# Early log sums on TensorE, exponentials for three more chunks, half products and pairwise weight sums in a fused SSD and expert kernel

## The chip, the cores and the metric

The kernel runs on one core of a Trainium2 chip. The metric is the device time of one execution in microseconds. A core has TensorE (PE, matmuls into PSUM banks), VectorE (DVE), ScalarE (ACT), GpSimd (POOL) and SyncE (SP), which issues nearly all DMA transfers here. Each engine takes its instructions in program order and waits for semaphores of the others.

## The reference

Four batches with eight heads of 768 tokens go through a Mamba2 state-space layer (chunks of 32 in the reference). Its output, 3072 tokens of 256 values, goes through four experts whose outputs are weighted by normalised probabilities:

```python
for c in range(nc):
    cum = np.cumsum(log_a[:, :, sl], axis=-1)
    L = np.exp(cum[:, :, :, None] - cum[:, :, None, :]) * causal
    M = np.einsum('bhin,bhjn->bhij', Cc, Bc) * L
    y_intra = np.einsum('bhij,bhjd->bhid', M, xc)
    y_inter = np.einsum('bhin,bhnd->bhid', Cc, state) * np.exp(cum)[:, :, :, None]
    y[:, :, sl] = y_intra + y_inter
    decay_from_j = np.exp(cum[:, :, -1:] - cum)
    state = np.exp(np.sum(la, -1))[..., None, None] * state + np.sum(
        np.einsum('bhjn,bhjd->bhjnd', Bc, xc) * decay_from_j[..., None, None], axis=2)
# tokens (3072, 256); p = domain_probs / sum
for e in range(4):
    out += p[:, e:e + 1] * (np.maximum(x @ w1[e], 0) @ w2[e])    # w1 256x1024, w2 1024x256
```

## The kernel before

Everything is fp32. The sequence is cut into chunks of 128 tokens, 24 in all: chunk c belongs to batch c mod 4, so c = 0 to 3 are the first chunks of the four batches and carry no earlier state, and six chunks (three pairs) make a block of the expert stage, four blocks in all. For each chunk the kernel needs the decays L between all pairs of its tokens and per head, the scores C·B, their product MT, and then `inner` (L546), which multiplies MT with the chunk's values and at the same time makes the chunk's part of the state. `score` is L502.

Decays are made in two ways. `scan` (L519, DVE) multiplies the a's up along the tokens against an identity: every row starts at its own token. It is used for c < SCANNED = 6; for chunks 0 to 2 the a's are spread over the partitions by matmuls of ones (`spread`, L660), for 3 to 5 they are read from DRAM, broadcast, into `ab` (L463, from `acut_d`). From chunk 6 on `decay` (L526, ACT) takes exponentials of differences of running log sums: `ab` is then read from `cum_d`, the negated sums per partition are in `neg`, and `causal` (L531, POOL) clears the upper triangle. `fade` multiplies B with the decays to the chunk's end. The DVE multiplications of scores and decays are L681 in the opening and L856 later.

The experts are computed with fewer products than a plain matmul: the four weight blocks of an expert (256 hidden columns each) and two halves of the input against a block's three pairs of chunks by a scheme of 20 products (`G`) per expert and layer, a unit of the order, and a scheme of 7 (`B`) for the first block's pairs 1 and 2. The weight operands of a scheme are sums and differences of weight blocks (`operands`, L1024, on POOL or DVE), stored to DRAM when first made (`w_d`, L1029) and read back for later blocks. Token operands are L1043 sums; the middle step (relu and gate) is `gated` (L968); L1071 adds a kept term into a bank; L942 and L947 copy between banks and SBUF; L1213 saves output banks; L1260 and L1425 add output terms. All product matmuls are L933; a product with 256 columns is two matmuls, and a matmul leaves two records in the trace. The first chunk pair is multiplied plainly for the four blocks of expert 0 (`plain_first`), because weight sums are not ready yet.

The order of work is fixed when the program is built. The opening (until about 13 us) is written out by hand: chunks 0 and 1, gates, the store of `acut_d`, the loads of the first weights, the log sums by a scan over time (L725) and the store of `cum_d`. Behind it a planner (`Plan.run`) goes through TensorE's list of work in the order given and puts the other engines' work in order by estimated costs, with a choice of DVE or POOL for sums and with SP's DMA issues. Constants such as `now = 13.2` and the ready times in `plan.taken` tell it when the opening is over. `PAIRS_AT` says where in a block's units the next block's chunk pairs get their scores (s) and outputs (o). At the end the last block's output pieces are turned on TensorE (L1325) and written out.

## Time and profile before

| | |
|---|---|
| median of 3 runs | 612.55 us (612.52 to 612.58) |
| the profiled execution's own time | 612.72 us |
| its span, first to last instruction | 610.9 us |
| TensorE busy | 603.7 us, 3365 records |
| VectorE, ScalarE, GpSimd busy | 489.8, 292.9, 158.8 us |
| product matmuls L933 | 1676 + 692 + 208 records |
| POOL weight sums L1024, 128x256 | 94 + 32, 794 and 763 ns each |
| DMA moved | 99.65 MB, mean 163 GB/s |
| granted TensorE clock | 1.00 |

A row of the timeline has start, length, engine, line, operation, tiles written and read, shape, count, and in brackets how long the engine stood idle before it and what ended that. Matmul records overlap; spacing between starts tells more than the length of one.

### The profile page before, as it was taken

What the parts mean: (1) busy time and instruction counts of PE and PEld (TensorE: products, weight loads), DVE (VectorE), ACT (ScalarE), POOL (GpSimd) and SP (SyncE); (2) the same over time, 40 slices, a digit from 0 to 9 for tenths busy, and PEclk for the clock granted to TensorE, in tenths of its full rate; (3) what the DMA queues carried; (4) which work ended last, traced back from release to release, by engine and by line L of the source; (5) the groups of instructions that cost most, each with busy time, mean ns of one, the idle gap of its engine ahead of it and who ended that gap; (6) DMA issues with size and microseconds to landing.
All of it is one profiled execution on the core that took longest, in us unless ns stands there. A gap on an engine that the chain in (4) does not pass through costs nothing.

```text
span 610.9 us, 10142 instructions
## 1 busy us (share of the span) xinstructions
PE 603.7 (99%) x3365; PEld 513.6 (84%) x3365; DVE 489.8 (80%) x854; ACT 292.9 (48%) x681; POOL 158.8 (26%) x238
## 2 busy tenths in 40 slices
PE   9999999999999999999999999999999999999997
PEld 5778778888888888888888888888888888888885
DVE  7899997988879894887969988396785989575775
ACT  5267365487642327868352334734444142434441
POOL 6565546556461001676400100200000000000000
PEclk9999999999999999999999999999999999999999
DMA  7757668566853429893332425863142232953001
GB/s 253 257 185 222 194 215 326 187 213 228 285 160 98 113 36 328 280 313 124 134 117 87 149 47 140 274 237 118 55 127 80 87 91 63 341 187 121 1 0 53
DMA packets 89060, 99.65 MB, mean 163 GB/s; under 512 B 27428, under 2 KB 58928, under 8 KB 89008
## 3 DMA queue, kind: packets, MB, share of 16 engines
q1 hardware_dynamic: 88852, 98.95, 51.3%
q8 instruction: 27, 0.44, 0.3%
q14 instruction: 25, 0.20, 0.1%
q10 hardware_dynamic: 156, 0.06, 0.0%
HBM read 78.80 MB, written 20.17 MB: 162 GB/s over the span
## 4 chain that ended last, share of the span: by engine, by line
PE 92%; DVE 2%; ACT 1%; issue 0%; DVEq 0%
PE bank L933 88%; PE bank L546 2%; PE bank L502 1%; PE bank L879 1%; ACT A L556 1%; DVE v L968 1%; DVE v L960 0%; DVE MT L856 0%; ACT v L894 0%; DVE bank L1071 0%; DVE v L1260 0%; PE bank L1325 0%; DVE v L1425 0%; ACT LT L894 0%; ACT v L1330 0%
## 5 line engine op out<-in xcount | busy, mean ns | idle before, releaser
L933 PE MATMUL bank<-v,w 128*128 128x256 f32 x1676 | 394.8, 380 | 0.8 <-DVE bank L1071 0.7
L933 PEld LDWEIGHTS bank<-v,w 128*128 128x128 f32 x1676 | 316.9, 190 | 48.2 <-issue 2.2
L933 PE MATMUL bank<-Y,w 128*128 128x256 f32 x692 | 177.6, 381 | 0.7 <-ACT LT L894 0.4
L1213 ACT COPY v<-bank 128x512 f32<-128x512 f32 x109 | 64.0, 587 | 178.5 <-PE bank L933 166.2
L933 PEld LDWEIGHTS bank<-Y,w 128*128 128x128 f32 x692 | 130.2, 190 | 22.4 <-issue 2.0
L968 DVE SCALAR_TENSOR_TENSOR v<-bank,gate 128x512 f32<-128x512 f32 x149 | 102.3, 688 | 42.6 <-PE bank L933 39.7
L960 DVE TENSOR_TENSOR v<-v,v 128x512 f32<-128x512 f32 x181 | 126.6, 719 | 1.7 <-ACT v L942 0.3
L1071 DVE TENSOR_TENSOR bank<-bank,v 128x512 f32<-128x512 f32 x84 | 57.4, 696 | 35.7 <-PE bank L933 23.4
L942 ACT COPY v<-bank 128x512 f32<-128x512 f32 x100 | 58.6, 587 | 54.0 <-PE bank L933 45.0
L1024 POOL TENSOR_TENSOR w<-w,w 128x256 f32<-128x256 f32 x94 | 73.1, 794 | 42.5 <-DVE v L960 14.5
L947 ACT COPY bank<-v 128x512 f32<-128x512 f32 x127 | 74.0, 595 | 10.7 <-DVE v L968 8.7
L933 PE MATMUL bank<-LT,w 128*128 128x256 f32 x208 | 52.7, 379 | 0.0
L526 ACT ACTIVATE MT<-ab,neg 128x128 f32<-128x128 f32 x144 | 47.1, 396 | 2.1 <-DMA ab<-cum_d 2.1
L933 PEld LDWEIGHTS bank<-LT,w 128*128 128x128 f32 x208 | 39.4, 190 | 5.3
L531 POOL TENSOR_SCALAR_AFFINE_SELECT MT<-MT 128x512 f32<-128x512 f32 x36 | 23.2, 655 | 69.2 <-ACT MT L526 53.9
L1024 POOL TENSOR_TENSOR w<-w 128x256 f32<-128x256 f32 x32 | 24.3, 763 | 18.8 <-DVE Y L1043 7.7
L960 DVE TENSOR_TENSOR v<-bank,v 128x512 f32<-128x512 f32 x26 | 17.9, 688 | 11.1 <-PE bank L933 9.9
L856 DVE TENSOR_TENSOR MT<-bank,MT 128x512 f32<-128x512 f32 x36 | 22.7, 681 | 0.1
L1260 DVE TENSOR_TENSOR v<-v,v 128x256 f32<-128x256 f32 x55 | 21.1, 422 | 1.0 <-ACT v L1213 0.7
L960 POOL TENSOR_TENSOR v<-v,v 128x512 f32<-128x512 f32 x6 | 7.7, 1277 | 49.7 <-DVE v L960 49.7
L968 DVE SCALAR_TENSOR_TENSOR v<-v,gate 128x512 f32<-128x512 f32 x26 | 19.8, 763 | 0.4
L495 ACT ACTIVATE ctm<-xb,tmask 128x128 f32<-128x128 f32 x48 | 15.8, 395 | 3.8 <-DMA xb<-in_xbc_dram 3.7
(110 smaller groups left out, 315.1 us busy)
## 6 DMA issues: line engine op xcount, KB each, us to landing
w<-w_d SPq DMA_DIRECT2D x128, 256.0 KB
w_d<-w SPq DMA_DIRECT2D x64, 256.0 KB
w<-in_w_dram SPq DMA_DIRECT2D x40, 256.0 KB
ab<-cum_d SPq DMA_DIRECT2D x18, 512.0 KB
w<-in_w_dram SPq DMA_DIRECT2D x64, 128.0 KB
gate<-p_d SPq DMA_DIRECT2D x15, 384.0 KB
xb<-in_xbc_dram SPq DMA_DIRECT2D x17, 192.0 KB
out_dram<-v SPq DMA_DIRECT2D x144, 16.0 KB
```

The source lines that it names most:

```text
L526: nc.scalar.activation(out=MT[:, place(c, h), 0:P], in_=ab[:, h * P:h * P + P], func=AF.Exp, bias=neg[:, h % NT, NQ * real(c) + h // NT:NQ ...
L531: nc.gpsimd.affine_select(out=MT[:, h:h + n, 0:P], in_=MT[:, h:h + n, 0:P], compare_op=ALU.is_ge, fill=0.0, base=0, pattern=[[0, n], [1, P ...
L856: nc.vector.tensor_mul(to, g, LT0[:, js, h] if cs[0] < SCANNED else to)
L933: nc.tensor.matmul(out=o, lhsT=w[:, j], rhs=x if half is None else x[:, j], start=(start and j == 0), stop=(j == 1), skip_group_check=True)
L942: act(.5, lambda e: nc.scalar.copy(out=flat(v), in_=bank.t), reads=[bank], writes=[v])
L947: act(.54 if to - lo > FB else .32, lambda e: nc.scalar.copy(out=bank.t[:, lo:to], in_=flat(v)[:, lo:to]), reads=[v], writes=[bank])
L960: plan.add(engines, lambda e: (on(e).tensor_add if sign > 0 else on(e).tensor_sub)(flat(v), whole(x), whole(y)), reads=[x, y], writes=[v], ...
L968: dve(D512, lambda e: nc.vector.scalar_tensor_tensor(out=h.t, in0=whole(x).rearrange("p (j m) -> p j m", j=JJ), scalar=0.0, in1=g.t[:, 2 * ...
L1024: plan.add(B256, lambda e, r=r, x=x, y=y, sign=sign: (on(e).tensor_add if sign > 0 else on(e).tensor_sub)(view(r), view(x), view(y)), two= ...
L1071: dve(D512, lambda e: (nc.vector.tensor_add if sign > 0 else nc.vector.tensor_sub)(to.t, bank.t, whole(x)), reads=[x, bank], writes=[to])
L1213: act(.5, lambda e: nc.scalar.copy(out=flat(v), in_=bank.t), reads=[bank], writes=[v], hold=HOLD)
L1260: plan.add(engines, lambda e: (on(e).tensor_add if sign > 0 else on(e).tensor_sub)(o[1](), x[1](), y[1]()), reads=[v for v in vs if v is n ...
```

## The change

It has four parts.

- Log sums early. The logarithm of `a` is taken right after the clipping; TensorE turns it (`sum_logs`), multiplies it with an upper triangle of ones (`upto`), which gives the running sums in both layouts, and ACT copies them to `cum` and, negated, to `neg`. The stores of `acut_d`, `p_d` and `cum_d` now stand together on SP ahead of the weights of blocks 2 and 3. The scan for the log sums and the later turn (`bias`, L1360) are gone.
- Chunks 2, 3 and 5 take their decays from exponentials; chunk 4 keeps its scan (`SCANS = 4,`). The triangle of the first four heads of chunks 2, 3 and 5 is cleared on DVE by a minimum with a mask of 2 and 0 (`bound`), the other four heads on POOL as before; `fade` of chunks 2 to 5 goes to DVE, by half chunks. `ab` has four buffers instead of two, the `v` pool 33 instead of 35. `spread` serves chunks 0 and 1 only, both at the start.
- `first_half`: for weight blocks 0 and 1 the first plain product is made per chunk, 128 columns at a time; chunk 0's part comes before chunk 1's `inner`. All four plain products stand ahead of the scores of chunks 2 and 3.
- Weight sums of two operands at a time: a pair of sums with a common layout is one instruction of 512 columns (7 pairs and 2 single ones instead of 16). For that the weights are loaded by input half with two blocks next to each other (`load_pair`).

Planner constants and the place of one pair's scores (24 to 18) are changed as well.

```diff
-NV, NW = 35, 28
+NV, NW = 33, 28
...
-SCANNED = 6
 SCORED, OWN, LEAD, LEFT = 7, 4, 5, 3
-FILLED = 3
-HORIZON, OPENING, LOADED = 26.0, 80.0, 1.0
+SCANS = 4,
+FILLED, EARLY, FADE = 3, 4, "DVE"
+CUT = {(c, 0): "DVE" for c in range(2, 6)}
+HORIZON, OPENING, LOADED = 26.0, 80.0, -0.5
 ORDERS = (0, 1, 2, 3), (3, 1, 2, 0), (0, 1, 2, 3), (3, 1, 2, 0)
-PAIRS_AT = ((1, 24, "s0"), (2, 1, "o0"), (2, 1, "s1"), (2, 24, "s2"), (3, 1, "o12")), (
+PAIRS_AT = ((1, 18, "s0"), (2, 1, "o0"), (2, 1, "s1"), (2, 24, "s2"), (3, 1, "o12")), (
...
-G.sums = ((15, 13, 10, -1), (9, 11, 10, -1), (0, "a", 16, -1), (2, "c", 11, -1), (1, "c", 13, -1),
-          (14, 16, 13, -1), (3, "e", 10, -1), (7, 10, "c", -1), (18, "d", 10, -1), (17, "d", 16, -1),
-          (8, 16, 11, -1), (19, "a", 13, -1), (6, "a", 11, -1), (12, 13, "d", -1), (5, "e", 16, -1),
-          (4, 11, "e", -1))
+G.ends = ("a", "c"), ("d", "e")
+G.sums = (((15, 9), (13, 11), 10), (0, "a", 16), ((1, 2), "c", (13, 11)), ((14, 8), 16, (13, 11)),
+          ((18, 3), ("d", "e"), 10), (7, 10, "c"), ((17, 5), ("d", "e"), 16),
+          ((19, 6), "a", (13, 11)), ((12, 4), (13, 11), ("d", "e")))
...
-    def causal(MT, h, n):
+    def causal(e, MT, h, n):
+        if e == "DVE":
+            nc.vector.tensor_tensor(
+                out=MT[:, h:h + n, 0:P], in0=MT[:, h:h + n, 0:P],
+                in1=bound.unsqueeze(1).to_broadcast([P, n, P]), op=ALU.min)
+            return
...
+    upto = const.tile([P, P], FP32)
+    nc.gpsimd.memset(upto, 1.0)
+    nc.gpsimd.affine_select(
+        out=upto, in_=upto, compare_op=ALU.is_ge, fill=0.0, base=0, pattern=[[1, P]],
+        channel_multiplier=-1)
...
+    def first_half(bank, w, y, c):
+        for i in range(2):
+            for j in range(JJ):
+                nc.tensor.matmul(
+                    out=bank.rearrange("p (a m) -> p a m", a=2)[:, j, c * P:c * P + P],
+                    lhsT=w1_half(w, i)[:, j], rhs=y[:, i, c * P:c * P + P],
+                    start=(c == 0 and i == 0 and j == 0), stop=(i == 1 and j == 1),
+                    skip_group_check=True)
...
+    def sum_logs(bank):
+        n = NCH * NH // 2
+        turned_ = homes["W"][-3][:, :2 * n].rearrange("p (r i) -> p r i", r=2)
+        nc.scalar.activation(out=a_sb, in_=a_sb, func=AF.Ln)
+        for r in range(2):
+            nc.tensor.transpose(bank[:, r * n:r * n + n], a_sb[:, r], ident[:n, 0, :n])
+        yield
+        nc.scalar.copy(out=turned_, in_=bank[:, :2 * n].rearrange("p (r i) -> p r i", r=2))
+        nc.tensor.matmul(
+            out=bank[:, 2 * P:2 * P + 2 * n], lhsT=upto, rhs=turned_.rearrange("p r i -> p (r i)"),
+            start=True, stop=True, skip_group_check=True)
+        for r in range(2):
+            nc.tensor.matmul(
+                out=bank[:n, r * P:r * P + P], lhsT=turned_[:, r], rhs=upto,
+                start=False, stop=True, skip_group_check=True)
+        yield
+        nc.scalar.copy(out=homes["cum"][1], in_=bank[:n, :2 * P].rearrange("p (r s) -> p r s", r=2))
+        yield
+        nc.scalar.mul(
+            homes["neg"][0], bank[:, 2 * P:2 * P + 2 * n].rearrange("p (r i) -> p r i", r=2), -1.0)
+        yield
...
+    logs, turning = sum_logs(four[0]), turn_gates(four[1])
     idle(BANK[6])
     idle(BANK[7], 3)
     spread(0, four)
-    idle(BANK[6], 3)
+    spread(1, seven, 1)
     mask(0, ctm[0], xb[0])
+    mask(1, ctm[1], xb[1])
     score([0], ctm[:1], xb[:1], seven)
-    scan_quarters(0, LT[0], four, 0)
+    scan_quarters(LT[0], four, 0, 0)
+    idle(four[1], 1)
+    next(logs)
+    next(turning)
     aside(0, 0, seven[0])
+    next(logs)
     aside(0, 1, seven[1])
-    scan_quarters(0, LT[0], four, 1)
-    fade(0, MT[0], xb[0], LT[0])
-    mask(1, ctm[1], xb[1])
-    spread(1, four)
+    next(turning)
+    next(logs)
+    store_decays(nc.sync, acut_d, a_cut)
+    nc.sync.dma_start(out=p_d.rearrange("e c s -> c e s"), in_=p_sb)
+    store_decays(nc.sync, cum_d, homes["cum"][1])
+    for fb in range(2, 4):
+        load_w1(fb, homes["W"][fb])
+    for fb in range(2):
+        load_w2(fb, homes["W"][4 + fb])
+    for c in range(2, 4):
+        load_decays(c, homes["ab"][c - 2])
+    for fb in range(2, 4):
+        load_w2(fb, homes["W"][4 + fb])
+    next(logs)
+    scan_quarters(LT[0], four, 0, 1)
     for r in (2, 3):
         masked(0, r, MT[0], LT[0], seven[r], 0)
-    turn_gates(BANK[7])
-    nc.scalar.activation(out=a_sb, in_=a_sb, func=AF.Ln)
-    next_ = [BANK[4], BANK[0], BANK[1], BANK[6]]
-    scan_quarters(1, LT[1], four, 0)
-    score([1], ctm[1:], xb[1:2], next_)
-    aside(1, 0, next_[0])
-    y = BANK[7][:, :NT * (P + N)].rearrange("p (t s) -> p t s", t=NT)
+    fade(0, MT[0], xb[0], LT[0])
+    idle(four[2], 3)
+    score([1], ctm[1:], xb[1:2], four, (2, 3, 1, 0))
+    scan_quarters(LT[1], seven, 1, 0)
+    aside(1, 1, four[1])
+    y = seven[0][:, :NT * (P + N)].rearrange("p (t s) -> p t s", t=NT)
     for t in range(NT):
         inner(0, t, y[:, t], xb[0], MT[0], P + N, t == 0)
     nc.scalar.copy(out=yT0[:, :, 0:P], in_=y[:, :, 0:P])
     keep_state(0, A[0], y[:, :, P:])
-    scan_quarters(1, LT[1], four, 1)
+    spread_gate(seven[1], homes["gate"][0])
+    scan_quarters(LT[1], seven, 1, 1)
+    for fb in range(2):
+        first_half(seven[2 + fb], homes["W"][fb], yT0, 0)
...
-    now = 13.2
+    now = 12.5
...
+    for c in range(2, 4):
+        st[c]["ab"] = plan.taken("ab", c - 2, now - 2.0 + 1.5 * c)
...
+        made, early = {}, c < blocks[0].n
+        for h in range(0, NH, NQ) if c in SCANS else ():
+            made[h] = dve(1.15, lambda e, h=h: scan(
+                LT0[:, j], s["ab"].t[:, h * P:h * P + NQ * P], place(c, h) * P),
+                reads=[s["ab"]], part=[LTv[place(c, h) // NQ]], two=True)
+        for h in range(NH) if c not in SCANS else ():
+            made[h] = act(.30, lambda e, h=h: decay(
+                c, s["MT"].t[:, j], s["ab"].t, neg.t, h),
+                reads=[s["ab"], neg], part=[s["MT"]])
+            if early and place(c, h) < NQ:
...
+            e = CUT.get((c, h), "POOL")
+            w = made[h] if c in SCANS else plan.add({e: .72 if early else .85}, lambda e, h=h: causal(
+                e, s["MT"].t[:, j], place(c, h), NQ), part=[s["MT"]], two=e == "DVE",
+                behind=[made[x] for x in range(h, h + NQ)])
+            cut.append(w)
+            to = [w]
+            if early:
+                e = FADE
+                to.append(plan.add({e: .3 if e == "POOL" else .2}, lambda e, h=h: fading(e, h, NQ),
...
+    def load_pair(v, fbs, l, f, i):
+
+        e, fb = divmod(fbs[f], EPB)
         if l == 1:
-            return w1[e, i * P:i * P + P, f * FB:f * FB + FB]
-        return w2[e, f * FB:f * FB + FB, i * P:i * P + P].rearrange("(j p) m -> p j m", p=P)
+            nc.sync.dma_start(out=v.t, in_=w1[e, i * P:i * P + P, fb * FB:fb * FB + 2 * FB])
+        else:
+            nc.sync.dma_start(
+                out=v.t.rearrange("p (j m) -> p j m", m=P),
+                in_=w2[e, fb * FB:fb * FB + 2 * FB, i * P:i * P + P].rearrange("(j p) m -> p j m", p=P))
...
+            for r, x, y in scheme.sums:
+                if isinstance(r, tuple):
+                    plan.add(B512, lambda e, r=r, x=x, y=y: difference(e, both(r), both(x), both(y)),
+                             two=True, reads=[where[x], where[y]], part=[where[r]], lean=True)
+                else:
+                    plan.add(B256, lambda e, r=r, x=x, y=y: difference(e, view(r), view(x), view(y)),
+                             two=True, reads=[where[x], where[y]], part=[where[r]], lean=True)
...
+        if fb < len(halves):
+            b = halves[fb]
+            seq = [plan.add({"PE": .44}, lambda e: first_half(b.t, w.t, y.t, 1), reads=[w, y], writes=[b])]
+            return seq, gated(b, gate_of(0, fb), 0)
...
-    for seq, _ in plain[:2]:
+    for seq, _ in plain[:EARLY]:
         line.extend(seq)
-    bias()
     scores([2, 3])
-    for seq, _ in plain[2:]:
+    for seq, _ in plain[EARLY:]:
```

## Prediction, made before the changed kernel had run

> **What bounds the kernel now.** I read the page's busy times first, then the stretches, then TensorE's waits, then the timeline of the first 30 us. The page:
>
> ```profile
> span 610.9 us, 10142 instructions
> PE 603.7 (99%) x3365; PEld 513.6 (84%) x3365; DVE 489.8 (80%) x854; ACT 292.9 (48%) x681; POOL 158.8 (26%) x238
> ```
>
> TensorE (PE) is the bound, so only what takes work or idle time out of its stream can show. The stretches (busy us by engine) and TensorE's waits after the opening:
>
> ```profile
> 0.00:12.60 12.60, 11.41 (x87) 5.99 (x87) 9.38 (x30) 5.94 (x17) 7.75 (x23) 1.00 0.73 229
> 12.60:26.30 13.70, 13.59 (x102) 10.99 (x99) 11.03 (x17) 4.44 (x15) 9.06 (x14) 1.00 0.86 280
> 60.00:80.00 20.00, 19.31 (x119) 15.62 (x122) 18.46 (x33) 7.77 (x23) 10.98 (x20) 1.00 0.66 206
> ```
> ```profile
> PE bank L1325 <- DVE v L1260: 0.7, 1, 0.7
> PE bank L933 <- DVE bank L1071: 0.7, 1, 0.7
> PE bank L933 <- ACT LT L894: 0.4, 1, 0.4
> ```
>
> Columns of the first: length, busy of PE, weight loads, DVE, ACT, POOL, granted clock, DMA share, GB/s. From 60 to 80 us VectorE (DVE) is busy 18.46 of 20 us: TensorE's losses there come from a full DVE queue. A product record (each fp32 product matmul leaves two) goes by every 0.216 us: groups of four start at 65.66, 66.53 and 67.39. Against that, the product runs lose about 1.0 us in all between 32 and 55 us in many small steps, 0.85 at 72 (the L1071 wait), 0.5 at 82 (the L894 wait), and 0.3 each at 123 and 232. From 233 us to the output's turns at 601 the stream is dense. So apart from the first 26 us some 3 us could be won.
>
> The beginning, from the timeline (start, length):
>
> ```profile
> 9.10 0.70 PE L546 MATMUL bank<-MT,xb 128*32 128x144 f32 x16
> 9.73 0.97 PEld L652 LDWEIGHTS bank<-p_sb,ident 96*128 96x128 f32 x8 [0.23 <-DVE LT L519]
> 10.82 1.21 PE L546 MATMUL bank<-MT,xb 128*32 128x144 f32 x16
> 11.21 0.47 SPq L463 DMA_DIRECT2D ab<-acut_d  x1
> 11.83 0.51 ACT L734 COPY v<-bank 128x128 f32<-128x128 f32 x2 [0.32 <-PE bank L546]
> 11.99 0.33 SPq L630 DMA_DIRECT2D cum_d<-cum  x1
> 12.61 3.72 PE L933 MATMUL bank<-v,w 128*128 128x256 f32 x16
> 16.16 0.33 PE L1360 MATMUL bank<-ident,cum 96*128 96x96 f32 x2
> 17.50 7.17 PE L933 MATMUL bank<-v,w 128*128 128x256 f32 x32
> 19.22 2.34 DVE L519 TENSOR_TENSOR_SCAN LT<-ab,ident 128x512 f32<-128x512 f32 x2 [2.06 <-DMA ab<-acut_d]
> 19.46 1.83 SPq L469 DMA_DIRECT2D ah<-cum_d  x3
> 24.68 1.69 PE L546 MATMUL bank<-MT,xb 128*32 128x144 f32 x32
> ```
>
> Chunk 1's own product ends near 11.9, ScalarE (ACT) copies it until 12.34, plain products run from 12.61. The loads are slow: `ab`, issued at 11.21, releases the scan at 19.22 (8.0 us); the `cum_d` store, issued at 11.99, releases its reader at 19.46 (7.4 us). Before `ab` the queue got 3.7 MB (eight weight tiles of 0.26, four chunks of 0.33, small ones of 0.3) and moved 229 GB/s at first.
>
> **The opening, part by part.** DVE's chain (eight scans of 0.6, five multiplications of 0.37, 4.68 to 11.30) keeps its length. New on TensorE, ACT and SP is the way to `cum_d` by logarithm, turn, triangular product and copy. The logarithm (0.42) overwrites what POOL still copies until 6.20: 6.25 to 6.7. Hand-overs ACT to PE take 0.26 (12.34 to 12.60), PE to ACT 0.35 from the last start (7.79 to 8.14). So: two turns 6.95, copy 7.4 to 7.7, product (a 192-column pass pair 0.33, four 96-row passes of 0.11) 8.0 to 8.7, copy 9.0 to 9.4, `cum_d` issued at 9.4 instead of 11.99, negated sums ready at 9.65. Chunk 1's scores now wait for those sums' bank: they end about 10.2 instead of 9.1, so chunk 0's product starts near 10.2, not 9.10. Its copy ends at 11.3. The first half products follow: eight passes of 128 columns each, by the L652 row 0.97/8 = 0.12 a pass, so 0.9 each, 1.8 for two: 11.5 to 13.3. Chunk 1's product 13.5 to 14.05, copies to 14.45, and the planned stream begins at 14.4.
>
> What TensorE then no longer has to do before the products of chunks 2 and 3: the turns at 16.16 (0.26) and 1.8 of plain products, done already. The `spread` of chunk 2 (11.96) lay under ACT's copy and its loss is worth nothing. The stream reaches L546 of chunks 2 and 3 after 0.9x2 + 16x0.216 (3.46) + scores 1.3 + 16x0.216 (3.46): 14.4 + 10.0 = 24.4, against 24.68. Without a wait it leaves at 25.5 (32 records in 1.12 later on, 1.62 here) instead of 26.30: 0.8 us at best.
>
> **The exponentials.** Chunks 2 and 3 now need `ab` from `cum_d`: store, landing, two loads of 512 KB behind four weight loads on SP's in-order queue. Of the store's 7.4 us now, 1.45 MB then in the queue (4.2 less 229x12.0) account for 4.4 at 330 GB/s; the other 3.0 stay. At 9.4 us here 229x9.4 covers the 2.1 MB issued, but the rate is lower at first, so 0.5 for a rest: the store is through at 12.9 and the loads follow; bounds 10.3 (0.5 after its issue) and 16.8 (7.4 again). Then ACT: four exponentials of chunk 2, four of chunk 3, chunk 3's mask, eight more; a run of five at L526 took 1.58 us, so 0.32 each, 1.3 for four. Behind T1, the landing of chunk 3's `ab`, lie 1.3 + 0.65 + 1.3 + 1.3 on ACT, POOL's L531 select 0.65, a fade on DVE 0.25, two multiplications 1.35 and TensorE's 1.16: 8.0 us. L546 leaves at T1 + 8.0. Bounds of T1: 3.2 MB lie ahead of the first load (six weight tiles, four chunks, 0.34 of small ones); by 12.6 us 229x12.6 = 2.9 MB have moved, the rest (0.3 MB plus two loads of 0.52) at 330 GB/s takes 4.1 us: data through at 16.7. (330 is 280 from 12.6 us on over a DMA share of 0.86.) The `ab` of before had 4.2 MB with its own, so by the same rates data through at 16.5, and it released its scan 2.7 later. T1 is 17.2 (tail 0.5, little more than a semaphore's hand-over) to 19.4 (tail 2.7), if the store does not hold the issue. I take 18.3, the middle, since the queue is shorter at the moment of issue (12.9): L546 leaves at 26.3, the 26.30 of now. Term: **0**, bounds -0.8 and +1.1.
>
> The Trainium skill (DMA: Bandwidth & Descriptors, Anatomy of one DMA) has a fixed cost of about 2 us plus bytes at 436 GB/s; by that the store would be through at 11.9, both loads by 16.4, and this term would be -0.8. Both rows above, 8.0 and 7.4 us, contradict it here, since others are queued ahead. The page's section Queues, rings and completion order says that a completion mark is written behind every earlier write of its engine, which speaks for the long tail of 2.7 and keeps the first rival's chance up.
>
> Weight tiles 2 and 3 of the first layer move from 7.2 behind `cum_d`, to about 10: with 2.7 us of tail they are there by 15.5, and TensorE asks at 16.2. The last two of the second layer come behind both `ab` loads, 0.52 MB or 1.5 us later, by 21; they are asked for at 25.5. ACT stands in order, so the masks and loads of chunks 4 and 5 wait behind the exponentials; chunk 5's exponentials and masks end about 26.5, TensorE needs them at 29.1, and six product matmuls (2.6) cover that. POOL waits in its order for chunk 2's last exponentials (about 21.5) with four weight sums behind; POOL is busy 6.7 of the 13.7 us after 26.3, which catches up; its next sums are needed after 36.
>
> **The middle.** DVE loses scans of chunks 2, 3 and 5 (2.43 + 2x2.34) and two log scans (0.73): 7.8 us. It gains three minima of 128x512 (nearest row L960: 0.72; bounds 0.4 and 1.2), eight fades of some 0.2 and 0.2 for chunk 4 and 5's multiplications taken singly: 4.0. Net 3.9 less before 33 us, and a good part where DVE stood waiting for `ab` anyway (2.06 before 19.22). Weight sums: on POOL 126 of 0.78 (97 us) become 29 of that and 49 of 512 columns at 1.28 (L960 on POOL): 85; on DVE 18 of 0.41 become 3 of that and 7 of 0.72: 1.1 less. POOL is 26% busy, so alone this is worth nothing; it frees POOL earlier to take a sum from DVE. The scores of block 1's first pair go in six products earlier, so DVE's four multiplications no longer stand before the L1071 sum that TensorE waited for. Of 1.0 + 0.85 + 0.5 I take half of the first, the whole of the second and a quarter of the third: **-1.5**; bounds -2.35 (all) and +1.0 (the first two as large again elsewhere, as six moved products have different neighbours, and two buffers fewer in V). Loads of weights in pairs move the same bytes; the issues saved on SP lie beside TensorE's stream. After 233 us nothing is left to win but the 0.7 at L1325, in the last turns, which the change leaves alone.
>
> **Sum.** 0 - 1.5: span 609.4, with the 1.8 us around it (612.72 - 610.94) 611.2; the profiled run is 0.17 above the median of 612.55, so 611.0.
>
> **Rivals.**
> - *Store holds loads* (slower). If `cum_d` takes 7.4 us as it did, the loads are issued at 16.8, not 12.9; T1 moves from 18.3 to about 21.8 and L546 leaves at 29.8: +3.5 - 1.5, 614.5. From T1 = 19.8 on the gain is gone. For it: the row itself; against: that store had over 4 MB ahead, this one 2.1.
> - *Early landing, all middle stalls gone*: -0.8 - 2.35, 609.4. For it: the freed DVE; against: two loads with 8.0 and 7.4 us.
> - *The stalls only move*: DVE still 18 of 20 us busy, the new order pays them at other products: 612.5. The change then does what it says, at the wrong place. For it: the net DVE saving lies before 33 us, mostly in idle time.
>
> **How the numbers follow.** Forecast 0.45 (own range 609.9 to 612.2, two thirds of it below 611.33, which is 612.55 less 0.2%), store 0.22, early 0.17, moved 0.16. A measurement tells about 0.2%, 1.2 us, from no change. Faster 0.30 + 0.17, same 0.15 + 0.16, slower 0.22. The range reaches over both outer cases: 609.0 to 614.5.
>
> **What would show it.** First planned product near 14.4; `cum_d` issued near 9.4, `ab` near 12.9; chunk 3's exponentials start at 18.3; L546 of chunks 2 and 3 leaves near 26.3; no DVE wait at L1071's successor near 72. I am wrong if the stream starts before 13 or after 15.5, if T1 is over 19.8, or if TensorE's waits between 30 and 130 us grow.

## The result, and the profile after

The changed kernel takes 615.22 us (median of 6 runs, 613.70 to 616.07) against 612.62 us for the kernel before on the same chip (612.52 to 612.73): a ratio of 1.0039, 95% interval 1.0025 to 1.0052. It is slower by 2.6 us. Three of its six runs, 615.56 us and above, show a granted clock of 0.997, the others, 614.88 and below, 0.999 or 1.000 (the last section comes back to this). The profiled execution took 614.88 us with a span of 613.2 us, 2.2 us more than before. First its page, span and busy times:

```profile
span 613.2 us, 10055 instructions
PE 602.8 (98%) x3377; PEld 513.5 (84%) x3377; DVE 488.9 (80%) x845; ACT 299.2 (49%) x707; POOL 155.6 (25%) x196
```

TensorE is busy 0.9 us less than before, in a span that is 2.2 us longer: its idle time grew by 3. Where, the stretches say (length, then busy us of PE, weight loads, DVE, ACT, POOL, granted clock, DMA share, GB/s), and under them TensorE's waits after the opening:

```profile
0.00:12.60 12.60, 10.87 (x81) 6.52 (x82) 8.23 (x27) 6.49 (x18) 8.77 (x26) 1.00 0.69 208
12.60:26.30 13.70, 11.47 (x86) 9.16 (x84) 7.22 (x16) 8.44 (x31) 5.55 (x8) 1.00 0.99 318
40.00:60.00 20.00, 19.38 (x85) 15.27 (x84) 17.38 (x32) 15.19 (x39) 10.79 (x12) 1.00 0.52 159
60.00:80.00 20.00, 19.79 (x102) 16.61 (x102) 17.20 (x29) 8.57 (x24) 12.68 (x20) 1.00 0.65 220
```
```profile
PE bank L502 <- ACT ctm L495: 2.1, 1, 2.1
PE bank L1433 <- DVE v L1368: 0.7, 1, 0.7
PE bank L1017 <- ACT LT L978: 0.4, 1, 0.4
PE bank L1017 <- DVE v L1052: 0.3, 1, 0.3
PE bank L1017 <- ACT v L1321: 0.2, 1, 0.2
PE bank L1017 <- DVE v L1044: 0.2, 1, 0.2
```

The kernel before, from 40 to 60 us:

```profile
40.00:60.00 20.00, 19.93 (x88) 15.80 (x88) 18.91 (x32) 15.87 (x41) 11.69 (x17) 1.00 0.78 235
```

Between 12.6 and 26.3 us TensorE is busy 11.47 of 13.70 us, where it was 13.59. The wait of 2.1 us is the scores (L502) of chunk 3, which wait for its mask (L495) on ACT. The wait of 0.7 us at 72 us (L1071 before) is gone, and from 60 to 80 us 0.5 us is won; but three small waits are new, and from 40 to 60 us 0.55 us is lost. (Lines after: products L1017, `inner` L551, `gated` L1052, combinations of V values L1044, `adjust`, which adds a kept term into a bank, L1175, weight sums L1077, minimum L532, multiplication L940.) The timeline of the opening (start, length):

```profile
9.10 0.35 SPq L639 DMA_DIRECT2D cum_d<-cum  x1
9.98 0.70 PE L551 MATMUL bank<-MT,xb 128*32 128x144 f32 x16
11.17 2.05 PE L726 MATMUL bank<-v,w 128*128 128x128 f32 x16
11.86 0.82 SPq L463 DMA_DIRECT2D ab<-cum_d  x2
13.99 1.86 PEld L726 LDWEIGHTS bank<-v,w 128*128 128x128 f32 x16 [0.44 <-ACT v L793]
18.90 2.70 ACT L526 ACTIVATE MT<-ab,neg 128x128 f32<-128x128 f32 x8 [3.97 <-DMA ab<-cum_d]
21.50 0.68 ACT L495 ACTIVATE ctm<-xb,tmask 128x128 f32<-128x128 f32 x2
22.09 2.43 ACT L526 ACTIVATE MT<-ab,neg 128x128 f32<-128x128 f32 x8
22.23 0.71 PE L502 MATMUL bank<-ctm,xb 32*128 32x256 f32 x8 [2.09 <-ACT ctm L495]
24.58 0.71 POOL L536 TENSOR_SCALAR_AFFINE_SELECT MT<-MT 128x512 f32<-128x512 f32 x1 [0.52 <-ACT MT L526]
26.53 1.73 PE L551 MATMUL bank<-MT,xb 128*32 128x144 f32 x32
```

The two `ab` loads are requested at 11.86 and 12.25 us, but ACT's first exponential starts only at 18.90, released by the load; the first of chunk 3 starts at 20.32 (inside the group of eight). The trace says what a landing is: the load's semaphore counts 16 parts, and the 16 come between 15.76 and 18.79 for the first load, between 18.02 and 20.23 for the second. The last part decides. The mask of chunk 3 stands behind those eight in ACT's order, and TensorE waits for it. `inner` of chunks 2 and 3 starts at 26.53 and the next product at 28.19: 1.89 us after the 26.30 of before.

From there on nothing moves. The long run of 320 product records after 120 us starts at 123.13 (121.23 before, +1.90), and the last ACT copy of output ends at 609.62 (607.74, +1.88). The other 0.33 us lie in the last transfers: 3.54 us from that copy to the end instead of 3.21.

So three marks are read in every run below: the end of chunk 2 and 3's `inner` ("leaves"), the *middle* (from there to the start of the 320-record run, 94.93 us before and 94.94 after), and the median.

### The profile page after: what moved, and what is told of

It is laid out like the page before. It is cut to its first block, busy times and chain, and to the rows that moved or that the text cites. A ratio compares the mean times of both kernels' runs of the same rounds, so it can differ in the third digit from the quotient of the medians.

```text
span 613.2 us, 10055 instructions
## 1 busy us (share of the span) xinstructions
PE 602.8 (98%) x3377; PEld 513.5 (84%) x3377; DVE 488.9 (80%) x845; ACT 299.2 (49%) x707; POOL 155.6 (25%) x196
## 4 chain that ended last, share of the span: by engine, by line
PE 91%; DVE 3%; DMA 2%; ACT 2%; POOL 1%; issue 1%; SPq 0%; DVEq 0%; ACTq 0%
PE bank L1017 87%; PE bank L551 2%; PE bank L502 2%; DMA ab<-cum_d 1%; DVE v L1044 1%; DVE v L1052 1%; PE bank L963 1%; ACT A L561 1%; ACT MT L526 1%; DVE bank L1175 1%; DMA cum_d<-cum 0%; DMA pr<-in_probs_dram 0%; POOL w L1077 0%; ACT v L978 0%; DVE v L1368 0%
## 5 line engine op out<-in xcount | busy, mean ns | idle before, releaser
L1017 PE MATMUL bank<-v,w 128*128 128x256 f32 x1592 | 377.7, 380 | 0.7 <-DVE v L1052 0.3
L1017 PEld LDWEIGHTS bank<-v,w 128*128 128x128 f32 x1592 | 301.0, 190 | 45.8 <-issue 3.3
L1017 PE MATMUL bank<-Y,w 128*128 128x256 f32 x692 | 177.5, 381 | 0.8 <-ACT LT L978 0.4
L1017 PEld LDWEIGHTS bank<-Y,w 128*128 128x128 f32 x692 | 130.2, 190 | 22.2 <-issue 1.5
L1044 DVE TENSOR_TENSOR v<-v,v 128x512 f32<-128x512 f32 x185 | 136.1, 751 | 2.4 <-ACT v L1026 0.9
L1052 DVE SCALAR_TENSOR_TENSOR v<-bank,gate 128x512 f32<-128x512 f32 x144 | 98.8, 688 | 34.4 <-PE bank L1017 31.1
L1077 POOL TENSOR_TENSOR w<-w,w 128x512 f32<-128x512 f32 (+1 forms) x74 | 82.0, 1118 | 48.5 <-DVE v L1044 12.5
L1175 DVE TENSOR_TENSOR bank<-bank,v 128x512 f32<-128x512 f32 x85 | 58.1, 696 | 34.0 <-PE bank L1017 22.9
L1031 ACT COPY bank<-v 128x512 f32<-128x512 f32 (+1 forms) x127 | 73.5, 590 | 11.5 <-DVE v L1052 6.0
L1017 PE MATMUL bank<-LT,w 128*128 128x256 f32 x276 | 69.8, 379 | 0.0
L1017 PEld LDWEIGHTS bank<-LT,w 128*128 128x128 f32 x276 | 52.4, 190 | 7.1
L940 DVE TENSOR_TENSOR MT<-bank,MT 128x512 f32<-128x512 f32 x40 | 25.3, 682 | 1.6 <-PE bank L502 1.4
L1044 DVE TENSOR_TENSOR v<-bank,v 128x512 f32<-128x512 f32 x27 | 18.6, 688 | 9.0 <-PE bank L1017 7.5
L1317 ACT COPY LT<-bank 128x512 f32<-128x512 f32 x12 | 7.0, 586 | 28.0 <-PE bank L1017 25.2
L1052 DVE SCALAR_TENSOR_TENSOR v<-v,gate 128x512 f32<-128x512 f32 x27 | 20.3, 753 | 0.4
L1052 DVE SCALAR_TENSOR_TENSOR LT<-bank,gate 128x512 f32<-128x512 f32 x18 | 12.4, 688 | 9.4 <-PE bank L1017 7.8
L502 PE MATMUL bank<-ctm,xb 32*128 32x256 f32 x192 | 14.4, 404 | 2.1 <-ACT ctm L495 2.1
```

Source lines behind the costliest of these rows:

```text
L502: nc.tensor.matmul(out=views[r][:, j], lhsT=xb[j][k, OBT:OBT + P], rhs=ctm[j][k].rearrange("p t s -> p (t s)"), start=(j == 0), stop=True, ...
L940: nc.vector.tensor_mul(to, g, to)
L1017: nc.tensor.matmul(out=o, lhsT=w[:, j], rhs=x if half is None else x[:, j], start=(start and j == 0), stop=(j == 1), skip_group_check=True)
L1031: act(.54 if to - lo > FB else .32, lambda e: nc.scalar.copy(out=bank.t[:, lo:to], in_=flat(v)[:, lo:to]), reads=[v], writes=[bank])
L1044: plan.add(engines, lambda e: (on(e).tensor_add if sign > 0 else on(e).tensor_sub)(flat(v), whole(x), whole(y)), reads=[x, y], writes=[v], ...
L1052: dve(D512, lambda e: nc.vector.scalar_tensor_tensor(out=h.t, in0=whole(x).rearrange("p (j m) -> p j m", j=JJ), scalar=0.0, in1=g.t[:, 2 * ...
```

## The experiments

The number behind "before" is the median of the kernel before in the same batch.

**The opening.** Five runs on what holds the exponentials.

*e1_mask_early*: the mask of chunk 3 is made in the opening, ahead of the exponentials.

```diff
     mask(2, ctm[0], xb[2])
+    mask(3, ctm[1], xb[3])
```

> The changed kernel with chunk 3's mask made in the opening, next to chunk 2's, so that it no longer stands behind the eight exponentials on ACT; the planned order of everything else is the same. Theory 'landing' (the late broadcast loads set when the product of chunks 2 and 3, L551, can end, whatever TensorE does before): the 2.1 us wait before the scores vanishes and comes back in front of L551; the exponentials run 0.7 earlier behind the mask, so L551 leaves at 27.5 instead of 28.19 and the time falls by 0.6, to about 614.6. Rival 'order on ACT' (the mask's place alone costs the time): L551 leaves near 26.0 and the time falls by 2.1 to 2.4, to about 613.0.

Measured: 613.66 us (before 612.47; ratio 1.0022, 1.0013 to 1.0032). The scores' wait is gone, but `inner` now waits inside itself:

```profile
24.38 0.50 PE L551 MATMUL bank<-MT,xb 128*32 128x144 f32 x4
26.13 1.17 PE L551 MATMUL bank<-MT,xb 128*32 128x144 f32 x28 [1.25 <-POOL w L1079]
27.23 0.70 PE L1019 MATMUL bank<-v,w 128*128 128x256 f32 x2
```

It is reached at 24.38 and leaves at 27.23 instead of 28.19. (The releaser named, a weight sum, is only the last event; the multiplications behind the exponentials end just before.) Of the 0.96 us won, 0.54 are the chain behind chunk 3's first exponential, which takes 7.33 us without the mask in it instead of 7.87; the other 0.42 are that exponential itself, which starts at 19.90 in this profile instead of 20.32, and the mask's place does not explain that. 0.93 above before remain. (How far such marks repeat: with the opening of before, `inner` leaves at 26.06 to 26.73 in seven profiles; with the changed opening and the early mask, at 27.17 to 27.42 in e1, e10 and e12.)

*e2_ab_first*: both `ab` loads ahead of all four second-layer weight tiles; *e3_both*: the two edits together.

```diff
-    for fb in range(2):
-        load_w2(fb, homes["W"][4 + fb])
     for c in range(2, 4):
         load_decays(c, homes["ab"][c - 2])
-    for fb in range(2, 4):
+    for fb in range(4):
         load_w2(fb, homes["W"][4 + fb])
```

> The changed kernel with the two broadcast loads issued ahead of all four second-layer weight tiles instead of behind two of them. Theory 'landing': 0.52 MB less lie ahead, at 330 GB/s 1.6 us: exponentials start near 17.3 instead of 18.9, the wait before the scores falls from 2.1 to 0.5, L551 leaves near 26.6, time falls by 1.6 to about 613.6. Rival 'fixed delay' (the loads take their 7 us from issue whatever is ahead, as the store and the load of the kernel before did): no change, 615.2.

> Both of these edits. Theory 'landing': L551 leaves near 26.0, time falls by 2.2 to about 613.0, still over the 612.6 of the kernel before. Rival 'order on ACT': as without the earlier loads, about 613.0 as well, but with exponentials starting at 18.9 as before; the start of the exponentials tells the two apart. Rival 'fixed delay': 614.6.

Measured: 615.27 us (1.0049, 1.0032 to 1.0066) and 614.16 us (1.0026, 1.0016 to 1.0036), leaving at 28.59 and 28.07. With half a megabyte less ahead of them chunk 2's exponentials start at 17.04 in e2, near the 17.3 of the theory, but at 19.33 in e3; chunk 3's start at 20.79 and 20.86, later than the 20.32 of the changed kernel. The 16 parts of the second load land between 18.16 and 20.70 in e2 and between 16.72 and 20.77 in e3: the first ones came earlier, the last ones did not. Two stretches of e2 (last column GB/s):

```profile
13.00:15.00 2.00, 1.86 (x27) 1.46 (x26) 0.09 (x1) 1.18 (x6) 0.00 (x0) 1.00 0.77 217
15.00:17.00 2.00, 2.00 (x15) 1.87 (x15) 1.78 (x4) 0.00 (x0) 1.41 (x2) 1.00 0.78 145
```

While the broadcast loads run almost alone, the queue moves 145 to 217 GB/s; in the trace their 4096-byte packets take 256 and 313 ns each (mean of the first and the second load) against 209 and 202 in the changed kernel. The place in the queue was won and the rate lost; why the packets take longer there was not tried.

*e4_ab_from_input*: mask early, and the two `ab` loads read the input `a` ahead of the stores, so that they wait for nothing. *e9_input_same_place*: the same source, requested where the changed kernel does. (The edit of e4; in e9 the two lines stand behind the second-layer weight tiles 0 and 1.) In both the decays of chunks 2 and 3 are not the reference's.

```diff
+    for c in range(2, 4):
+        nc.sync.dma_start(out=homes["ab"][c - 2], in_=a[real(c)].rearrange(
+            "h s -> (h s)").partition_broadcast(P))
     store_decays(nc.sync, acut_d, a_cut)
```

> Chunk 3's mask in the opening, and the broadcast loads of chunks 2 and 3 read the input a itself, before the stores, so that they wait for nothing (the decays of these two chunks are then not the reference's; everything else is computed). Theory 'landing': exponentials start when ACT is free, near 15, L551 is reached at 24.1 and leaves near 25.3, 2.9 earlier than in the changed kernel: about 612.3; what then remains against the kernel before is the middle, where the same stalls were paid at other products. Rival 'order on ACT': 613.0, as with the mask moved alone. If the time falls below 611.5, the middle is worth more than the trace of the changed kernel says.

> The changed kernel with the early mask, and the two loads of the decays of chunks 2 and 3 read from the input array at the same place in the queue as in the changed kernel, behind the stores (the decays of those two chunks are not the reference's). It tells the place of the request from what it reads. Theory (the place in the queue and the transfer set the landing): requests at 11.5 to 12.2 as before, exponentials start at 18.0 to 19.0, L551 leaves at 26.7 to 27.4, 613.1 to 613.9 as in the run with the mask alone. Rival (rows that have only just been written are slow to read, or the wait for the store costs): exponentials start before 17.0, L551 leaves by 26.2, 612.3 to 612.9.

Measured: e4 612.39 us (before 612.47; 1.0002, 0.9991 to 1.0013), leaving at 25.61, level with the kernel before; its exponentials start at 15.07, when ACT is free. (In its profile the run of 320 starts at 120.22, 1.0 us before that of the kernel before, and the last transfers take 0.5 of it back; the medians differ by 0.1.) e9 614.19 us (before 612.56; 1.0035, 1.0021 to 1.0049): requests at 11.57 and 12.08, exponentials from 18.23, leaving at 27.42, as e1. So neither the source nor the wait for the store matters much, but when the loads are requested and what the queue then moves. The stretches 11 to 13 and 15 to 17 us, of e4 and then of the changed kernel:

```profile
11.00:13.00 2.00, 2.00 (x19) 1.96 (x19) 0.67 (x3) 1.85 (x7) 1.53 (x4) 1.00 1.04 381
15.00:17.00 2.00, 2.00 (x16) 1.89 (x15) 1.69 (x4) 1.97 (x8) 1.42 (x2) 1.00 1.09 375
```
```profile
11.00:13.00 2.00, 2.00 (x19) 1.96 (x18) 0.39 (x2) 1.17 (x5) 1.39 (x4) 1.00 0.88 235
15.00:17.00 2.00, 2.00 (x16) 1.87 (x15) 1.78 (x4) 0.00 (x0) 1.42 (x2) 1.00 0.95 287
```

From 9 to 19 us the queue moved 3.64 MB in e4, 3.48 before, 3.00 in the changed kernel. What lowers the rate to 235 GB/s right behind the stores stays open: in e4 the packets of the `p_d` store pass between 13 and 15 us, a stretch that moved 353 GB/s.

**One load moved in the kernel before.** *e7_load_first* requests chunk 3's decays ahead of the four weight tiles; *e15_both_loads_first* also moves chunk 5's, with the planner's order kept: it goes ahead of the four weight loads that stood before it (second part of the edit).

```diff
+    load_decays(3, homes["ab"][0])
     for fb in range(4):
         load_w2(fb, homes["W"][4 + fb])
-    load_decays(3, homes["ab"][0])
...
+    late = [done[i] for i in queue[-4:]]
+    done.insert(done.index(scans[3]) + 1, done.pop(x))
+    for w in late:
+        done.remove(w)
+    x = done.index(early[5]) + 1
+    done[x:x] = late
```

> The kernel before, with the decays of chunk 3 requested ahead of the four second-layer weight tiles instead of behind them. Theory (the landing of that load is what DVE waits for from 17.2 to 19.2 us, and it costs TensorE 0.5 us before L546): the scan starts 1 to 2 us earlier, L546 takes 1.1 instead of 1.6 us and leaves at 25.8, and 612.0 results. Rival from the run with both loads first: bytes ahead in the queue do not set the landing, the scan starts at 18.5 or later and the time is that of before, 612.5. Second rival: the weight tiles, now behind, come too late for the product after L546: 612.6 to 613.5.

> The kernel before with the planner's order kept on every engine, and two loads moved by hand on SP's queue: the decays of chunk 3 ahead of the four second-layer weight tiles, as in the run with that load first, and the decays of chunk 5 ahead of the four weight tiles that stood before it (it was issued at 24.60 there). Theory: chunk 5's scan starts by 28.5 instead of 29.96, the two waits of 0.4 and 0.5 us at L879 and before it are gone, 36 us is reached 0.4 us earlier than before, 612.0 to 612.4. Rival (the first 35 us are bound by what the queues move, so that what goes first only makes something else late): another wait of 0.4 us or more before 37 us, 612.6 to 614.

Measured: e7 614.30 us (before 612.56; 1.0031, 1.0018 to 1.0043). The first gain came, then something else was late:

```profile
17.28 3.17 DVE L519 TENSOR_TENSOR_SCAN LT<-ab,ident 128x512 f32<-128x512 f32 x2
...
29.96 1.22 DVE L519 TENSOR_TENSOR_SCAN LT<-ab,ident 128x512 f32<-128x512 f32 x1 [1.84 <-DMA ab<-acut_d]
```

Chunk 3's scan starts 1.94 us earlier and `inner` leaves at 25.93, but chunk 5's scan now waits 1.84 us for its load, and TensorE loses 0.9 us at 33 to 35 us. e15 mends that (scan at 28.47, no wait of TensorE between 16 and 37 us), and its median is 612.54 us, that of before (612.54; 0.9998, 0.9989 to 1.0007). Its opening happened to reach the first planned product 0.6 us later than in the profile of before, and kernels with the same opening spread by as much (first `inner` at 9.10 to 9.77 us), so a gain of half a microsecond is neither shown nor excluded.

**The middle.** Its parts one by one. *e5_pairs_alone*: the kernel before with the pairs. *e8_begun_at_18*: the kernel before with the moved scores. *e17_pairs_and_18*: both. *e6_begun_at_24*: the changed kernel without the move. *e10_no_pairs_18*: the changed kernel with the early mask, without the pairs. The core of the pairs (put in in e5 and e17, taken out in e10) and the move (put in in e8 and e17, taken back in e6):

```diff
+G.ends = ("a", "c"), ("d", "e")
-G.sums = ((15, 13, 10, -1), (9, 11, 10, -1), (0, "a", 16, -1), ...
+G.sums = (((15, 9), (13, 11), 10), (0, "a", 16), ((1, 2), "c", (13, 11)), ...
...
-PAIRS_AT = ((1, 24, "s0"), ...
+PAIRS_AT = ((1, 18, "s0"), ...
```

> The kernel before, with nothing but the weight sums made two at a time and the raw weights loaded in pairs. Theory: sums and loads lie beside a TensorE stream that is dense from 26 us on, so what they save on POOL and DVE is worth nothing; the 0.85 us loss at 72 us stays: 612.1 to 612.9, L546 leaves at 26.3 as before, and 123 us is reached at the same time to within 0.4 us. Rival, the forecast's middle step: a freer DVE and POOL take at least half a microsecond of the small losses between 32 and 82 us: 611.9 or less. Second rival: the pairs themselves bring the new losses at 47 to 62 us of the changed kernel (1.5 us): 613.5 or more.

> The kernel before, with nothing but the scores of the second block's first pair put behind 18 products instead of 24. Theory (the move takes the 0.85 us loss at 72 us, and the new losses at 47 to 62 us of the changed kernel came with the pairs): opening as before (L546 leaves at 26.3), 123 us is reached 0.5 to 0.9 us earlier, 611.6 to 612.1. Rival (the losses only move): 612.4 to 613.0, with new losses of about 0.85 us between 44 and 66 us.

> The kernel before with both parts of the change that lie after the opening, the pairs and the scores behind 18 products, and its own opening (scans, no exponentials for chunks 2, 3 and 5). Theory (the two parts fit only each other, and the freed DVE has little to do with it): from the end of chunks 2 and 3's own products to the long run of products after 120 us it takes 94.4 to 95.2 us, as in the changed kernel and in the kernel before (94.9), instead of 97.0 with the pairs alone and 100.7 with the move alone; 612.2 to 613.0. Rival (the DVE work that the exponentials save is needed as well): over 95.6 us for that stretch, 613.4 or more.

> The changed kernel, with the scores of the second block's first pair of chunks put back behind 24 products instead of 18. Theory (the losses only move): the loss of 0.85 us near 72 us is back, and the new ones at 47 to 62 us (1.48 us in all) go to less than half, so that the time stays that of the changed kernel to within 0.5 us: 614.5 to 615.6. Rival (the forecast's view: the move is worth 0.85 by itself and the new losses come from other parts): 615.9 or more, with both the old and the new losses in the trace.

> The changed kernel with the early mask, without the pairs: weight sums of 256 columns and raw weights loaded as before. Theory (the pairs cost some 2 us by themselves, of which the move of the scores and the freed DVE hid the larger part): opening as in the run with the mask alone (L551 leaves at 27.2), and the stretch from there to the products after 120 us 0.8 to 2 us shorter than in that run: 611.7 to 612.9. Rival (the pairs are neutral in the changed kernel): 613.4 to 614.0, the time of the run with the mask alone.

| kernel | middle, us | median, us | ratio to before (95%) |
|---|---|---|---|
| before | 94.93 | 612.5 to 612.7 | 1 |
| pairs alone (e5) | 97.03 | 615.13 | 1.0040 (1.0027 to 1.0052) |
| move alone (e8) | 100.74 | 617.35 | 1.0072 (1.0058 to 1.0085) |
| pairs and move (e17) | 96.19 | 614.37 | 1.0028 (1.0019 to 1.0038) |
| changed, without the move (e6) | 99.77 | 619.20 | 1.0112 (1.0090 to 1.0134) |
| changed with early mask, without the pairs (e10) | 100.99 | 620.76 | 1.0131 (1.0117 to 1.0145) |
| changed | 94.94 | 615.22 | 1.0039 (1.0025 to 1.0052) |
| changed with early mask (e1) | 94.48 | 613.66 | 1.0022 (1.0013 to 1.0032) |

Along before, e5, e17 and the changed kernel, the zero of the middle is a sum: the pairs add 2.10, the move on top of them takes 0.84, the rest of the change (with the DVE work that the exponentials save) takes 1.25. But no part has one price. The move takes 4.8 in the changed kernel and adds 5.8 alone; the pairs, taken out of the changed kernel with the early mask, leave the middle 6.5 longer. e8 and e10 share a loss that neither parent has, a wait of 3.7 and 3.8 us for an `adjust` that ends at 114 and 117 us, with a spell at half clock behind it (last section); e6 waits 2.6 us at 58 us, 0.6 at 81 us, which is the old wait of 72 us, and has two such spells. My expectations for e5, e8 and e10 were wrong on that point, e6 lies beyond its rival, and e17 fell on the rival's side.

What the pairs do is seen in e5's timeline:

```profile
51.20 1.27 POOL L993 TENSOR_TENSOR w<-w,w 128x512 f32<-128x512 f32 x1 [0.69 <-DVE v L960]
51.58 1.44 DVE L960 TENSOR_TENSOR v<-v,v 128x512 f32<-128x512 f32 x1
52.94 0.69 DVE L1091 TENSOR_TENSOR bank<-bank,v 128x512 f32<-128x512 f32 x1
...
53.78 0.45 PE L933 MATMUL bank<-Y,w 128*128 128x256 f32 x1 [1.01 <-DVE bank L1091]
```

A DVE sum of two SBUF operands (0.68 us on its own) that meets a POOL weight sum of 512 columns takes 1.44 us; the `adjust` behind it is late, and TensorE waits 1.01 us for that bank. In the whole kernel such DVE sums of 512 columns that took over 1.2 us number 3 before, 13 with the pairs alone, 18 in the changed kernel. The Trainium skill (SBUF — State Buffer, section SBUF: two separate sides) says that DVE and GpSimd share one pair of ports as an exclusive lock for a whole instruction; the lengths above agree.

*e11_pool_in_halves* and *e12_mask_and_halves* tried whether it is the length of POOL's instruction: same order, each sum of two on POOL as two instructions of 256 columns, in e5 and in e1.

```diff
-difference(e, both(r), both(x), both(y))
+[difference(e, both(r)[:, s], both(x)[:, s], both(y)[:, s])
+ for s in ((slice(0, 1), slice(1, 2)) if e == "POOL" else (slice(0, 2),))]
```

> The kernel before with the pairs, its order of work unchanged, but each sum of two that falls to POOL issued as two instructions of 256 columns (0.72 us each) instead of one of 512 (1.27 us). Theory (a DVE sum of two SBUF operands that meets a POOL sum stands until POOL's instruction has ended, so that doubling POOL's instruction doubles the hold): DVE sums of over 1.2 us fall from 17 to under 10, the two waits at L1091 (2.2 us together) to under 1.3, and 613.0 to 614.2 results instead of 615.1. Rival (it is the new order of sums and loads, not the length of an instruction): 614.6 to 615.7, as with the pairs alone.

> The changed kernel with the early mask, its order of work unchanged, and the sums of two on POOL issued as two instructions of 256 columns. Theory (hold by POOL's longer instruction): the losses at 47 to 55 us (1.1 us in the run with the mask alone) fall by a third to two thirds: 612.9 to 613.4. Rival (order, not length): 613.4 to 614.0, the time of the run with the mask alone.

Measured: 614.37 us (before 612.55; 1.0030, 1.0019 to 1.0042), middle 96.74, 0.29 less than e5; and 614.61 us (1.0037, 1.0023 to 1.0050), middle 94.62, 0.14 more than e1. Sums over 1.2 us fall from 13 to 10 in e11 and from 18 to 9 in e12, but TensorE's two waits for an `adjust` are 2.4 us together in e11, 2.2 in e5. The same place in e11:

```profile
50.69 3.07 POOL L993 TENSOR_TENSOR w<-w,w 128x256 f32<-128x256 f32 x3 [0.69 <-PE bank L933]
51.07 0.91 DVE L960 TENSOR_TENSOR v<-v,v 128x512 f32<-128x512 f32 x1
51.90 0.69 DVE L1092 TENSOR_TENSOR bank<-bank,v 128x512 f32<-128x512 f32 x1
...
52.73 1.10 PE L933 MATMUL bank<-Y,w 128*128 128x256 f32 x4 [1.24 <-DVE bank L1092]
```

The hold falls from 1.44 to 0.91 us here, and TensorE still waits, 1.24 us, for the same `adjust`. In e5 and e11 a sum of two V values (L960) stands ahead of that `adjust` in DVE's order; in the kernel before the `adjust` goes first, and TensorE does not wait:

```profile
50.89 0.68 DVE L1071 TENSOR_TENSOR bank<-bank,v 128x512 f32<-128x512 f32 x1
51.49 2.73 DVE L960 TENSOR_TENSOR v<-v,v 128x512 f32<-128x512 f32 x4
```

So the longer holds are real, but shortening them gave back at most 0.29 of the 2.10; that the order around them is the larger part is argued from this place, not shown for the whole.

Is it the order as such, then? *e13_other_estimate* and *e14_other_horizon* change one number of the planner each (the first and the second of these edits), and no work; the planner then lays all later work in another order.

```diff
-    B512, B256 = {"DVE": D512, "POOL": 1.3}, {"DVE": D256, "POOL": .72}
+    B512, B256 = {"DVE": D512, "POOL": 1.3}, {"DVE": D256, "POOL": .74}
...
-HORIZON, OPENING, LOADED = 26.0, 80.0, 1.0
+HORIZON, OPENING, LOADED = 25.0, 80.0, 1.0
```

> The kernel before with one number of its planner changed and no work added, removed or resized: the planned time of a weight sum of 256 columns on POOL is 0.74 instead of 0.72 us. The planner lays all later work in another order. Theory (each order found by the planner has its own few losses, so that any edit that makes it plan anew moves the time by some us, whatever the edit is worth): the opening is as before (L546 leaves at 26.3), 123 us is reached over 0.8 us later or earlier, and 613.4 or more results; the median of the four edits that planned anew so far is 3.7 us above before. Rival (what the parts of the change do sets the time, the order as such does not matter): 612.2 to 612.9.

> The kernel before with another number of its planner changed and the same work: loads in the first 80 us are planned at most 25 us ahead of their need instead of 26. A second draw for the same question as the run with the other estimate: theory 613.4 or more with a loss of over 1 us at one place between 36 and 125 us that before does not have; rival 612.2 to 612.9.

Measured: 613.11 and 613.15 us (before 612.54; both 1.0010, 1.0001 to 1.0019), middles 95.22 and 95.33. The medians are 0.6 us above before, neither the 613.4 or more of the theory nor nothing. One and the same order spreads too: seven profiles with the order of the changed kernel (its own, e1 to e4, e9, e16) have middles of 94.46 to 95.02. So the 0.84 and 1.25 above are uncertain by about half a microsecond. The 2.1 of the pairs and the 5.8 of the move are well above that; how much of them belongs to the parts and how much to the order that the planner finds around them, two draws do not show.

**Two more.** *e16_kept_busy*: the changed kernel with four products with a zero matrix in TensorE's wait for the mask.

```diff
         for j, c in enumerate(cs):
+            for r in range(4) if j and cs[0] == 2 else ():
+                nc.tensor.matmul(
+                    out=views[r][:, j], lhsT=zero.to_broadcast([P, P]),
+                    rhs=ident[:, :NT], start=False, stop=True, skip_group_check=True)
```

> The changed kernel with four more products of 256 columns with a zero matrix on TensorE between the scores of chunk 2 and of chunk 3, in the 2.1 us in which it waits for chunk 3's mask. They add zeros, and 1.7 us of them lie in the wait. Theory (the changed kernel's runs spread over 2.4 us, and lie above its profiled run, because in some runs TensorE comes out of that wait at half its clock, as it did in the profile of the run with the scores behind 24 products, at 0.70): the spread falls below 1.2 us and the median to 613.9 to 614.6. Rival (the spread comes from the landing of the loads): spread over 2 us and median 615.0 to 615.8.

Measured: 614.42 us (613.91 to 615.43, 6 runs; 1.0033, 1.0021 to 1.0044). The median lies where the theory had it, the spread of 1.5 us between the two. None of these runs has a granted clock below 0.998, while three of the changed kernel's six have 0.997 and lie above the other three; in e1, without that wait, none of ten has. With the half clock behind this same wait in e6's profile, that speaks for the clock as a cause of the spread; what spreads e16's runs is another, and open.

*e18_pairs_18_load*: e17 with e7's moved load.

> The same with the decays of chunk 3 requested ahead of the four second-layer weight tiles; the order on the other engines is that of the run with both parts. In this order only two weight tiles stand ahead of chunk 5's decays on SP's queue. Theory (the 0.5 us wait before L546 goes and nothing else comes late): 0.3 to 0.6 us below the run with both parts, 611.6 to 612.5, a version that beats the kernel before. Rival (what goes first in the queue makes something else late, as in the two runs that moved loads): the same as the run with both parts to 0.2 us, or above it.

Measured: 615.69 us (before 612.66; 1.0051, 1.0038 to 1.0064). `inner` leaves at 25.87, but the middle grows to 97.98. No version beat the kernel before.

## Why the prediction was wrong, step by step

- *The opening on TensorE* was right. Store of `cum_d` at 9.10 (forecast 9.4), first halves at 11.17 (11.5), the second ones at 13.99 (14.4), `inner` of chunks 2 and 3 reached at 24.38 once the mask is out of the way (24.4), and without any wait it leaves at 25.61, in e4 (25.5).
- *The exponentials, term 0*, was the first step that failed, by its size: +1.89, outside its bounds of -0.8 and +1.1. The chain was right: behind chunk 3's landing it had 8.0 us, and 20.32 to 28.19 are 7.87. T1 was wrong: 20.32 instead of 18.3, beyond the 17.2 to 19.4 that I allowed. What failed is "data through at 16.7": the second load's last packet ends at 19.81. By 12.6 us 208x12.6 = 2.6 MB had moved, not 2.9; from 11 to 17 us 235 to 316 GB/s were moved, not 330; and by 19.81 some 0.4 MB of weight tiles requested behind the load had moved as well, while its last parts were still to come. The forecast took the bytes of a queue to pass in the order of the requests, and in this trace they do not. The tail from there to the exponential was 0.5 us, not 1.6, which hid 1.1 us of the miss. I also counted 0.65 us for the mask in the chain without asking who waits for it: TensorE stood 2.09 us before the scores, and the chain is 0.54 shorter with the mask early. By the Trainium skill (DMA: Bandwidth & Descriptors, Anatomy of one DMA) the term was to be -0.8, further off. From its fixed 2 us and its rate, which it gives for transfers issued by GpSimd while these are issued by SP, one would estimate 2.2 us for the store (here 2.8 from its issue to the next request) and 3.2 for a load (here 7.0 from request to use).
- *Store holds loads* gave the right sign, and its 614.5 comes near. That is luck: its mechanism did not happen (the loads were requested 2.8 us after the store, not 7.4), and it kept the -1.5 of the middle.
- *The middle, -1.5*, was the second failed step. The move did take the loss at 72 us: -0.84 on top of the pairs, for a forecast of -0.85. The rest gave -1.25 for -0.65. What failed is "alone this is worth nothing" for the pairs: put in first, they cost 2.10. I argued from POOL's share of busy time, 26%, and looked neither at what DVE does while a POOL sum of twice the length runs, nor at the order that results. DVE was to be busy 3.9 + 1.1 us less and was 0.9 less; its sums of two V values (L960, now L1044) took 751 instead of 719 ns each, 185 and 181 of them. That the parts could be priced one by one at all, from waits of the old order, failed too: taken out of the changed kernel, the pairs leave it slower.
- *The stalls only move* had the right middle, 0, and a part of the reason: DVE is still busy 17.38 of 20 us from 40 to 60 us, and the new waits there are DVE's. That the move alone would cost 5.8 it did not say.
- *The end*: 0.33 us in the last transfers, which I had left at nothing. In the eight profiles with exponentials, pairs and move together the last copy is followed by 3.4 to 3.7 us, in the other twelve by 3.1 to 3.2. Why was not tried.

Together 1.89 + 0.01 - 0.02 + 0.33 = 2.2 us, the growth of the profiled span. The 2.6 us between the medians hold the runs at clock 0.997 as well.

## What to carry to other kernels

Price a load that something waits for by the rate of the very stretch in which it runs and by the last of its 16 parts, not by its place in the queue, and ask what stands behind the waiting instruction on its engine: a mask of 0.58 us cost 0.54. An engine at 26% can still hold up another one (a DVE sum took 1.44 instead of 0.68 us); whether the bound engine pays for it depends on the order. And where a planner orders the work, parts of a change have no price of their own; compare whole orders, with a change of a mere estimate as the yardstick (here 0.6 us).

## What the runs showed of the hardware

A wait of TensorE can cost twice. In e8 it waits 3.66 us at 110 us for an `adjust`; the chain of e8 after that wait, and the stretches (granted clock in the third column from the right):

```profile
114.07 5.49 PE L933 MATMUL bank<-v,w 128*128 128x256 f32 x12 [3.66 <-DVE bank L1071]
```
```profile
110.00:114.00 4.00, 0.41 (x2) 0.01 (x1) 4.00 (x8) 1.18 (x2) 3.32 (x7) 0.89 0.37 127
114.00:120.00 6.00, 5.93 (x14) 4.78 (x15) 3.46 (x6) 0.99 (x3) 2.75 (x4) 0.51 0.35 99
120.00:126.00 6.00, 6.00 (x95) 4.82 (x98) 4.99 (x9) 1.08 (x2) 1.46 (x2) 1.00 0.48 147
```

For 5.8 us after it the clock is granted at 0.51 and a product record takes 0.427 instead of 0.216 us: another 2.9 us. The same followed a wait of 3.8 us in e10, and in e6 waits of 2.6 and even 2.1 us (clock 0.70 from 24 to 28 us); a wait as long as the last did not do it in the changed kernel's profile, nor one of 2.6 us in e2's. The granted clock in the traces tells when. It changes only on a grid of 3.41 us, and in all 20 profiles a stretch of that grid in which TensorE's matmul records leave 1.8 us or more idle is followed by one at half clock (14 stretches, ten of them at the kernel's end); where they leave 1.7 us or less, none is. So a wait of 2.1 us costs another 1.7 us (half of 3.41) or nothing, by where the grid cuts it. The Trainium skill (TensorE: Matmul & The Clock Gate, Part 1: The HAM clock gate) has the array at half its clock after an idle window of about 3.4 us that runs freely; a grid that runs freely fits that, but stretches idle for little more than half of it were enough here.
